# More warm-up products in the first head, fills behind the running sum, and new priorities in a planned attention and two-layer kernel

## The chip, the cores and the metric

The kernel runs on one core of a Trainium2 chip. The metric is the device time in microseconds (us) of one execution; lower is better. The engines are TensorE (PE, its weight loads PEld), VectorE (DVE), ScalarE (ACT), GpSimd (POOL) and SyncE (SP), which issues the DMAs.

## The reference

```python
def _attn_ref(q, k, v, s):                      # 4 batches, 8 heads, 576 positions, 64 per head
    scores = scale * np.matmul(q, k.transpose(0, 1, 3, 2))
    cum = np.cumsum(np.maximum(s, 0.0), axis=-1)
    bias = -(cum[:, :, :, None] - cum[:, :, None, :])
    scores = np.where(causal, -1000000000.0, scores + np.minimum(bias, 0.0))
    attn = np.exp(scores - np.max(scores, axis=-1, keepdims=True))
    attn = attn / (np.sum(attn, axis=-1, keepdims=True) + 1e-09)
    return np.matmul(attn, v)
# x: 2304 x 512
h = (x @ w1) * (x @ w2) @ w3;  y = h @ w_out    # 512 -> 1024 -> 512
h2 = y @ w_in;  out = (h2 - np.tanh(h2)) @ w_out2   # 512 -> 2048 -> 512
```

## The kernel before

**Stages.** Batch 0 comes first, its eight heads in plain fp32 (`full`). The 24 heads of the other batches work on fp32r pairs: a value is split into a high part (a copy) and a low part (a subtraction), and a product is three matmuls. The two products with w1 and w2 (`products`, six blocks of 384 tokens) are put between the heads as the results of whole batches come. Then w3 and w_out are multiplied into one weight matrix (`wah`, `wal`), which is applied to the tokens (the x2 stage), and last the layer with w_in, the tanh and w_out2 runs in blocks of 512 tokens (the last stage; 16 slices of the hidden size, f, in each).

**A head** has five query tiles (`QT`: 64 and four of 128 rows). For each: scores into one of two banks, a reduction on DVE that adds the mask and finds the maximum, an exponential on ACT, transposes on PE (`flip`), copies out of PSUM, and the product with v (`pv`). The bias enters as rows of the k side that hold the running sum relative to the tile's middle (`rel`): each head after the first gets them by DMA into `rqk`, five rows beside the 64 of k, and needs one matmul per piece. The first head multiplies q and k alone and adds the bias by a second matmul (ones by `rel`) into the same bank.

**The weights.** They arrive as 64-bit floats and are made into fp32 by one ACT step and four DVE steps for 128 x 512 values (`assemble`, lines 487 to 493), then split by a copy (line 385 on ACT, 386 on DVE) and a subtraction (389 on DVE, 391 on POOL). w1 and w2 are 16 such blocks. w_out2 is 16 more; four of them are assembled early, laid by in DRAM and fetched later (`lay_by`, `fetch`). Four blocks of w_out2 have room in the pool `pre`, which opens while the x2 stage still runs; the other twelve stand in `p2`, which opens when it ends.

**What sets the order.** A planner (`Plan.order`) gives each operation a start by its own estimates: at each moment an engine takes the ready operation with the smallest priority number, and operations that two engines can do (copies on ACT or DVE, subtractions on DVE or POOL) go where the planner expects the earlier end, with a handicap for each. The program is then written out in that order, and each engine runs its own list in order. All numbers of the table `PARAM` feed it: `convp` and `convq` are the priorities of the w1 and w2 blocks (a head's number is 100 times its place), `qk` and `kb` how early a head's loads are asked for, `dsub0`, `dcopy0` the handicaps of DVE for subtractions and copies in the first stretch. Where PE would stand idle before `fu`, the planner puts in warm-up products (`filler`: 128x128 bf16 on zeros, into a bank nobody reads).

## Time and profile before

| | |
|---|---|
| median of three runs | 961.36 us (957.67 to 964.69) |
| span of the profiled execution | 957.5 us; no other time of it is given, and the lowest run is 957.67 |
| PE busy | 941.5 us (98%) |
| DVE, ACT, POOL busy | 662.6, 594.8, 419.2 us |

The profile is one execution. A busy PE is not a PE at its peak, since the ends of matmuls are modelled: in the heads of batch 0, PE counts as busy nearly throughout but runs fewer matmuls in the same time than later. So the stretches are compared by several engines together, and with the granted clock.

### The profile page before, as it was taken

What the parts mean: (1) busy time and instruction counts of PE and PEld (TensorE: products, weight loads), DVE (VectorE), ACT (ScalarE), POOL (GpSimd) and SP (SyncE); (2) the same over time, 40 slices, a digit from 0 to 9 for tenths busy, and PEclk for the clock granted to TensorE, in tenths of its full rate; (3) what the DMA queues carried; (4) which work ended last, traced back from release to release, by engine and by line L of the source; (5) the groups of instructions that cost most, each with busy time, mean ns of one, the idle gap of its engine ahead of it and who ended that gap; (6) DMA issues with size and microseconds to landing.
All of it is one profiled execution on the core that took longest, in us unless ns stands there. A gap on an engine that the chain in (4) does not pass through costs nothing. (4 is left out here: it accounts for less than half of the span.)

```text
span 957.5 us, 15393 instructions
## 1 busy us (share of the span) xinstructions
PE 941.5 (98%) x5147; PEld 819.6 (86%) x5147; DVE 662.6 (69%) x1383; ACT 594.8 (62%) x1362; POOL 419.2 (44%) x337
## 2 busy tenths in 40 slices
PE   9997999999999999999999999999999999999998
PEld 5775999998999998899888887888888888888897
DVE  6998777678877579982588878894454544554555
ACT  4997677888898554441455468665555655655564
POOL 2445455645565254430687736453233233233321
PEclk7999999999999999999999999999999999999999
DMA  5655565565543145573598780121002101000010
GB/s 183 204 167 149 153 207 176 160 212 178 154 135 98 53 131 181 181 271 136 152 362 286 234 289 25 51 103 45 1 1 89 44 1 44 34 12 0 1 46 22
DMA packets 64305, 118.96 MB, mean 124 GB/s; under 512 B 6433, under 2 KB 34321, under 8 KB 64226
## 3 DMA queue, kind: packets, MB, share of 16 engines
q1 hardware_dynamic: 64226, 117.98, 38.6%
q8 instruction: 40, 0.66, 0.3%
q14 instruction: 39, 0.32, 0.1%
HBM read 88.81 MB, written 25.46 MB: 119 GB/s over the span
## 5 line engine op out<-in xcount | busy, mean ns | idle before, releaser
L391 POOL TENSOR_TENSOR gl<-pg,gh 128x512 fp32r<-128x512 f32 (+1 forms) x78 | 118.7, 1522 | 231.7 <-ACT gh L385 219.6
L933 PE MATMUL bank<-x2b,wih 128*128 128x512 f32 (+1 forms) x640 | 182.4, 370 | 0.0
L944 DVE TENSOR_TENSOR pg<-bank,u 128x512 f32<-128x512 f32 (+1 forms) x80 | 51.0, 637 | 138.9 <-ACT th L943 132.3
L933 PEld LDWEIGHTS bank<-x2b,wih 128*128 128x128 f32 x640 | 117.0, 188 | 22.1
L941 ACT ACTIVATE u<-bank 128x512 f32<-128x512 f32 (+1 forms) x80 | 44.4, 555 | 126.1 <-PE bank L933 125.9
L933 PE MATMUL bank<-x2b,wil 128*128 128x512 f32 (+1 forms) x320 | 117.9, 368 | 0.0
L956 PE MATMUL bank<-voh,gl 128*128 128x512 f32 x288 | 113.2, 393 | 1.7 <-POOL gl L391 1.6
L954 PE MATMUL bank<-voh,gh 128*128 128x512 f32 x288 | 113.0, 392 | 0.0
L955 PE MATMUL bank<-vol,gh 128*128 128x512 f32 x288 | 112.6, 391 | 0.0
L666 ACT ACTIVATE e<-e,nmx 128x320 f32<-128x320 f32 (+4 forms) x160 | 89.0, 559 | 16.0 <-DVE nmx L660 15.3
L698 PE MATMUL bank<-ident,e 128*128 128x128 f32 (+1 forms) x480 | 80.0, 278 | 3.9 <-ACT e L666 2.2
L660 DVE CUSTOM_DVE_ANT_0 e<-bank,msk 128x320 f32<-128x320 f32 (+4 forms) x160 | 65.8, 422 | 23.1 <-PE bank L650 13.4
L391 POOL TENSOR_TENSOR xl<-cf,xh 128x512 fp32r<-128x512 f32 (+1 forms) x40 | 55.3, 1409 | 47.4 <-ACT xh L385 45.1
L948 DVE COPY_PREDICATED pg<-mk,th 128x512 f32<-128x512 uint32 (+1 forms) x80 | 68.4, 856 | 8.5 <-ACT mk L946 1.4
L389 DVE TENSOR_TENSOR el<-bank,eh 64x64 fp32r<-64x64 f32 (+1 forms) x144 | 63.8, 458 | 12.1 <-ACT eh L385 11.3
L487 ACT ACTIVATE wt<-wraw 128x512 f32<-128x512 f32 x72 | 48.0, 669 | 34.6 <-DMA wraw<-w_out 13.0
L933 PEld LDWEIGHTS bank<-x2b,wil 128*128 128x128 f32 x320 | 60.2, 188 | 10.5
L493 DVE SCALAR_TENSOR_TENSOR wt<-wraw,wt 128x512 uint32<-128x512 uint32 x72 | 68.5, 953 | 0.9
L797 PE MATMUL bank<-xh,w1h 128*128 128x384 f32 x192 | 68.8, 358 | 0.1
L491 DVE SCALAR_TENSOR_TENSOR wt<-wraw,wt 128x512 uint32<-128x512 uint32 x72 | 67.5, 940 | 1.0
L797 PE MATMUL bank<-xh,w2h 128*128 128x384 f32 x192 | 67.6, 352 | 0.0
L698 PEld LDWEIGHTS bank<-ident,e 128*128 128x128 f32 (+1 forms) x480 | 56.5, 139 | 12.5 <-ACT en L385 2.8
(139 smaller groups left out, 2493.5 us busy)
## 6 DMA issues: line engine op xcount, KB each, us to landing
rqk<-qk SPq DMA_DIRECT2D x24, 576.0 KB
wraw<-w_out SPq DMA_DIRECT2D x24, 512.0 KB
c_d<-cst SPq DMA_DIRECT2D x48, 192.0 KB
wraw<-w SPq DMA_DIRECT2D x16, 512.0 KB
wraw<-w3t SPq DMA_DIRECT2D x16, 512.0 KB
wraw<-w_in SPq DMA_DIRECT2D x16, 512.0 KB
cf<-c_d SPq DMA_DIRECT2D x32, 256.0 KB
x_d<-x2s SPq DMA_DIRECT2D x16, 512.0 KB
```

The source lines that it names most:

```text
L391: o.append(("POOL", c_pool2(n), lambda: nc.gpsimd.tensor_tensor(dst(), a(), b().bitcast(F32), op=ALU.subtract)))
L491: dve(lambda: nc.vector.scalar_tensor_tensor(t_.t, h32(), 0xC0000000, t_.t, op0=ALU.bitwise_and, op1=ALU.bitwise_or), 512, [r_, t_], [t_], ...
L493: dve(lambda: nc.vector.scalar_tensor_tensor(t_.t, l32(), 29, t_.t, op0=ALU.logical_shift_right, op1=ALU.bitwise_or), 512, [r_, t_], [t_], ...
L660: nc.vector.tensor_tensor_reduce(e.t[:nq, EOFF[t] + k0:EOFF[t] + k1], bk.t[:nq, :k1 - k0], bi.t[:nq, bo + k0:bo + k1], -0.125, 3.0e38 if f ...
L666: act(lambda: nc.scalar.activation(et(), et(), AF.Exp, bias=nmx.t[:nq, i, tm:tm + 1], scale=-1.0, accum_out=ssum.t[:nq, pj, t, i:i + 1]), ...
L698: nc.tensor.transpose(bk.t[:rows, n * P:(n + 1) * P], e.t[:, EOFF[t] + c * P:EOFF[t] + c * P + rows], ident.t)
L797: nc.tensor.matmul(bk.t[:, :TB], w_.t[:, k, f * P:(f + 1) * P], x_.t[:, k, o:o + TB], start=k == 0 and i == 0, stop=k == KC - 1 and i == 2)
L933: nc.tensor.matmul(bk.t[:, :w], w_.t[:, k, a], X2.t[:, i, k, :w], start=k == 0 and n == 0, stop=k == KC - 1 and n == 2)
L948: dve(lambda pg=pg, mk=mk, th=th, c_=c_: nc.vector.copy_predicated(c_(pg), c_(mk).bitcast(U32), c_(th)), w, [mk, th], [pg], pr, two=True)
L954: nc.tensor.matmul(bank[n].t, gh.t[:, a], voh[f].t, start=f == 0, stop=False)
L955: nc.tensor.matmul(bank[n].t, gh.t[:, a], vol[f].t, start=False, stop=False)
L956: nc.tensor.matmul(bank[n].t, gl.t[:, a], voh[f].t, start=False, stop=f == NF2 - 1)
```

## The change

Five things. (1) `PARAM`: priorities and handicaps are other numbers, among them `convp` 581 to 1692.7 and `convq` 511 to 1648.5 (the w1 and w2 blocks rank behind the heads of batch 0), `lay0` 4 to 0 (slices 0 to 3 of w_out2 are laid by in DRAM, where it was 4 to 7) and `wlast` 12 to 6. (2) Warm-up products are planned at 55 ns where it was 107, and go into gaps from 60 ns where it was 110: 164 of them where it was 91. (3) Memory settings (`zero`) depend on the running sum, and the two of `rqk` are done by POOL. (4) The last two tiles of the first head take the bias as rows, like the other heads: their second matmuls go, and a DMA brings the rows. (5) The first half of the w1 and w2 blocks waits for the last of the five relative sums.

```diff
-PARAM = dict(ramp0=146, ramp1=-16.1, dsub=2038, dsub0=404, dcopy=753, dcopy0=203, dother=1000.0, dother0=1000.0, spi=420, lay=4, lay0=4, layp=2.2e5, layf=2.95e5, dve0=1000.0, early=140811, raw0=0, rawp=-700.0, ng=3, nosb=2, cut=(1,), convq=511, natb=8, wap=0.95e6, dve=1000.0, act=-188, pool=-128, sem=160.0, pesem=180.0, slow=1.1, convp=581, npre=4,
-             nbias=3, keep=0.5, ff=0.0, fu=174005, wlast=12, kbp=246, qk=-145, kb=-365, rv=116, st=9.8, fl=38, iv=174, pv=129, ml=-120, bw=370.0, ntr=3, actb=1, actn=0, spp=-44, ne=2, nsb=2, ncf=5, outlag=40)
+PARAM = dict(cst=1050.9, ramp0=113.5, ramp1=35.9, dsub=5134.3, dsub0=979.7, dcopy=723.0, dcopy0=29.4, dother=1000.0, dother0=1000.0, spi=1234.9, lay=4, lay0=0,
+             layp=263506, layf=214480, dve0=1000.0, early=154617, raw0=0, rawp=-700.0, ng=3, nosb=2, cut=(1,), convq=1648.5, natb=8, wap=842711, dve=1000.0,
+             act=-76.1, pool=-71.7, sem=160.0, pesem=180.0, slow=1.1, convp=1692.7, npre=4, nbias=3, keep=0.5, ff=0.0, fu=215099, wlast=6, kbp=469.5, qk=-461.8,
+             kb=-1288.7, rv=341.5, st=7.6, fl=112.8, iv=-82.0, pv=113.8, ml=-119.7, bw=370.0, ntr=3, actb=1, actn=0, spp=349.6, ne=2, nsb=2, ncf=5, outlag=119.8)
...
-                while self.fill_from < free[e] and free[e] + 110.0 < t < self.fill_until and not unread and free[e] >= read:
+                while self.fill_from < free[e] and free[e] + 60.0 < t < self.fill_until and not unread and free[e] >= read:
...
-                    f.dur = 107.0 * self.clock(free[e])
+                    f.dur = 55.0 * self.clock(free[e])
...
-    def zero(views, n, w, prio, value=0.0):
-        pl.op([("DVE", sum(0.521 * x + 75.0 for x in n), lambda: [nc.vector.memset(v_(), value) for v_ in views])], w=w, prio=prio, two=True)
+    def zero(views, n, w, prio, value=0.0, r=()):
+        pl.op([("DVE", sum(0.521 * x + 75.0 for x in n), lambda: [nc.vector.memset(v_(), value) for v_ in views])], r=r, w=w, prio=prio, two=True)
...
+    scan = [(rel, 5)]
...
+            zero([later(en, 1024, EN, low), later(en, 0, D, low)], [P, D], [en], 30, r=scan)
...
+            for R in rqk:
+                pl.op([("POOL", 560.0, lambda R=R: nc.gpsimd.memset(R.t[D:D + 5, S:], 0.0))], w=[(R, 2)], prio=-2300)
...
-            S, [(rel, 5)], [(rel, t)], -900 + t if t < 3 else 20.0 + t, fast=True)
+            S, [(rel, 5)], [(rel, t)], -900 + t, fast=True)
...
-        elif n_head[0] > 1:
-            for t0, t1 in ((0, 3), (3, 5)) if 1 in groups else ((0, 3),):
+        else:
+            for t0, t1 in ((3, 5),) if one else ((0, 3), (3, 5)) if 1 in groups else ((0, 3),):
...
-                    if one:
+                    if one and t < 3:
...
-                if one:
+                if one and t < 3:
...
-                        PARAM["convp"] + half * PARAM["convq"] + (2 * k + (src is w2)) * PARAM["ramp%d" % half], PARAM["rawp"] if half == 0 and 2 * k + (src is w2) < PARAM["raw0"] else None)
+                        PARAM["convp"] + half * PARAM["convq"] + (2 * k + (src is w2)) * PARAM["ramp%d" % half], PARAM["rawp"] if half == 0 and 2 * k + (src is w2) < PARAM["raw0"] else None,
+                        [(rel, 4)] if half == 0 and 2 * k + (src is w2) else [])
```

Line numbers of the changed kernel are up to five higher (the scores of later heads are 651 where they were 647), and the setup code has moved. Three places show what the planner makes of it.

PE, first head, from the third query tile to the first scores of the second head. Before: each piece of scores has a second matmul with `rel`; `rqk_103` holds the first head's q and k, `rqk_104` the second's; L698 are transposes, L738 the product with v.

```order
129 L644 MATMUL bank_58<-rqk_103 128x320
130 L645 MATMUL bank_58<-rel,e_114 128x320
131 L644 MATMUL bank_59<-rqk_103 128x448
132 L645 MATMUL bank_59<-rel,e_114 128x448
133 L698 MATMUL bank_61<-ident,e_113 64x128
134 L698 MATMUL bank_62<-ident,e_113 128x128 x2
135 L644 MATMUL bank_58<-rqk_103 128x288
136 L645 MATMUL bank_58<-rel,e_114 128x288
137 L644 MATMUL bank_59<-rqk_103 128x288
138 L645 MATMUL bank_59<-rel,e_114 128x288
139 L698 MATMUL bank_63<-ident,e_113 128x128 x3
140 L698 MATMUL bank_61<-ident,e_113 128x128 x4
```

Now (L548 is a warm-up product; of runs of them the last row stands here):

```order
214 L548 MATMUL bank_60<-msk 128x128
215 L648 MATMUL bank_58<-rqk_103 128x320
216 L649 MATMUL bank_58<-rel,e_114 128x320
217 L702 MATMUL bank_62<-ident,e_113 128x128 x2
218 L702 MATMUL bank_61<-ident,e_113 64x128
...
263 L651 MATMUL bank_59<-rqk_103 128x448
264 L651 MATMUL bank_58<-rqk_103 128x288
265 L702 MATMUL bank_63<-ident,e_113 128x128 x3
...
274 L651 MATMUL bank_59<-rqk_103 128x288
275 L742 MATMUL bank_60<-en,rv_106 80x320
...
278 L702 MATMUL bank_61<-ident,e_113 128x128 x4
279 L651 MATMUL bank_58<-rqk_104 128x64
```

The three second matmuls of the last two tiles are gone, 77 warm-up products stand ahead of the first scores (62 before), then 28 ahead of row 215, 22 ahead of row 263 and four ahead of row 274, and the second head's first scores come before the transposes of the first head's last tile.

DVE, the beginning. Before:

```order
8 L522 MEMSET rqk_103 5x576
...
10 L522 MEMSET rv_106 128x16
...
12 L522 MEMSET en 64x128
...
14 L571 TENSOR_SCALAR rel<-rel 32x576
15 L522 MEMSET e_114 128x64 x4
16 L572 SCALAR_TENSOR_TENSOR rel<-rel 32x576
...
18 L578 TENSOR_SCALAR rel<-rel 32x576 x3
19 L660 ISA e_113,nmx<-bank_58,msk 64x64
...
21 L578 TENSOR_SCALAR rel<-rel 32x576 x2
22 L660 ISA e_113,nmx<-bank_59,msk 128x192
```

Now:

```order
5 L524 MEMSET ssum 128x20
6 L555 TENSOR_SCALAR rel<-rel 32x576
7 L556 SCALAR_TENSOR_TENSOR rel<-rel 32x576
8 L582 TENSOR_SCALAR rel<-rel 32x576 x5
9 L524 MEMSET e_113 128x64 x4
10 L524 MEMSET en 64x128
...
12 L524 MEMSET e_113 64x64
13 L664 ISA e_113,nmx<-bank_59,msk 128x192
...
15 L664 ISA e_113,nmx<-bank_58,msk 64x64
```

The running sum (row 7) has no memory setting between it and its input, all five relative sums follow it at once, and the first reductions come behind them and behind four settings.

DVE, where the x2 stage ends and the last stage begins (`wt` is an assembled block of w_out2, `voh` its high part, L944 and L949 the first step of the last stage). Before, the cast is slice 8; slices 4 to 7 come by DMA:

```order
1024 L488 TENSOR_SCALAR wt_83<-wt_83 128x512
1025 L489 TENSOR_SCALAR wt_83<-wt_83 128x512
1026 L491 SCALAR_TENSOR_TENSOR wt_83<-wraw_81,wt_83 128x512
1027 L386 CAST voh_5697<-wt_82 128x512
1028 L944 TENSOR_TENSOR pg_5730<-bank_62,u_5724 128x512
```

Now the casts are slices 4 and 5, and slices 6 to 15 are all assembled behind this point:

```order
1024 L391 TENSOR_TENSOR x2s_4794<-bank_61,x2s_4794 128x256
1025 L388 CAST voh_5746<-wt_82 128x512
1026 L388 CAST voh_5747<-wt_83 128x512
1027 L949 TENSOR_TENSOR pg_5783<-bank_62,u_5777 128x512
...
1034 L490 TENSOR_SCALAR wt_82<-wt_82 128x512
```

On PE there, seven slices of the first product stand ahead of the first of the second, where it was six.

## Rows read from the trace of the kernel before

**Rows 1.** The page: span; busy time, share and instructions of each engine.

```profile
span 957.5 us, 15393 instructions
PE 941.5 (98%) x5147; PEld 819.6 (86%) x5147; DVE 662.6 (69%) x1383; ACT 594.8 (62%) x1362; POOL 419.2 (44%) x337
```

**Rows 2.** Windows: stretch, length, busy of PE, PEld, DVE, ACT, POOL, clock, DMA, GB/s.

```profile
11.84:22.08 10.24, 10.24 (x28) 5.30 (x26) 5.53 (x13) 5.11 (x13) 2.19 (x2) 0.50 0.41 104
22.08:81.94 59.86, 57.94 (x339) 43.59 (x338) 54.17 (x156) 53.88 (x157) 25.43 (x20) 1.00 0.63 186
81.94:97.17 15.23, 10.40 (x69) 8.45 (x68) 11.92 (x34) 11.24 (x38) 9.38 (x10) 0.89 0.40 107
97.17:340.00 242.83, 240.74 (x1732) 234.76 (x1730) 178.26 (x559) 192.00 (x542) 128.48 (x125) 1.00 0.50 151
560.00:600.00 40.00, 38.33 (x167) 30.66 (x166) 33.09 (x49) 31.95 (x57) 22.50 (x15) 1.00 0.39 133
600.00:957.50 357.50, 353.99 (x1637) 293.80 (x1635) 196.43 (x305) 202.06 (x380) 113.36 (x76) 1.00 0.09 33
```

**Rows 3.** Timeline of PE, first head: start us, length us, what, idle before.

```profile
6.49 0.32 PE L644 MATMUL bank<-rqk 64*64 64x64 f32 x2
...
9.67 0.80 PE L645 MATMUL bank<-rel,e 1*128 1x320 f32 x2
...
14.72 1.32 PE L645 MATMUL bank<-rel,e 1*128 1x288 f32 x2
...
20.34 2.03 PE L738 MATMUL bank<-en,rv 128*80 128x320 f32 x6
...
22.77 1.46 PE L647 MATMUL bank<-rqk 69*128 69x64 f32 x6
```

**Rows 4.** Timeline of DVE, first head.

```profile
5.27 0.33 DVE L522 MEMSET e<- 128x64 f32 x4
5.63 1.35 DVE L572 TENSOR_TENSOR_SCAN rel<-rel 32x576 f32<-32x576 f32 x1
...
8.74 0.94 DVE L578 TENSOR_SCALAR rel<-rel 32x576 f32<-32x576 f32 x2
...
16.46 1.34 DVE L389 TENSOR_TENSOR el<-rel,eh 64x1152 fp32r<-64x1152 f32 x1
...
18.59 0.52 DVE L660 CUSTOM_DVE_ANT_0 e<-bank,msk,nmx 128x288 f32<-128x288 f32 x1 [0.78 <-PE bank L645]
```

**Rows 5.** Groups of DVE, 0 to 81.94: count, busy us, mean ns, idle before.

```profile
L491 DVE SCALAR_TENSOR_TENSOR wt<-wraw,wt 128x512 uint32<-128x512 uint32 x16 | 12.0, 748 | 0.0
...
L488 DVE TENSOR_SCALAR wt<-wt 128x512 f32<-128x512 f32 x16 | 7.7, 488 | 0.8 <-ACT wt L487 0.5
```

**Rows 6.** Groups of ACT, 0 to 81.94.

```profile
L385 ACT ACTIVATE en<-bank 128x512 f32<-128x512 f32 (+3 forms) x47 | 17.6, 416 | 7.2 <-PE bank L698 4.5 <-PE bank L738 2.5
L487 ACT ACTIVATE wt<-wraw 128x512 f32<-128x512 f32 x16 | 10.6, 674 | 7.0 <-DMA wraw<-w 6.4 <-POOL w1l L391 0.5
```

**Rows 7.** Waits of PE over the whole span: total, times, longest us.

```profile
PE bank L698 <- ACT e L666: 2.2, 1, 2.2
PE bank L740 <- DVE el L389: 1.9, 1, 1.9
PE bank L956 <- POOL gl L391: 1.6, 1, 1.6
```

**Rows 8.** Timeline of DVE, 86 to 91.

```profile
87.15 2.58 DVE L389 TENSOR_TENSOR qs<-rqk,qs 64x320 fp32r<-64x320 f32 x1
```

**Rows 9.** Timeline of ACT, last stage: copies of a w_out2 block's high part.

```profile
588.84 0.64 ACT L385 ACTIVATE voh<-wt 128x512 fp32r<-128x512 f32 x1 [1.96 <-DVE wt L493]
...
640.72 0.63 ACT L385 ACTIVATE voh<-wt 128x512 fp32r<-128x512 f32 x1 [0.75 <-DVE wt L493]
```

**Rows 10.** Chain of waits, last stage: first product of two neighbouring slices.

```profile
590.04 2.75 PE bank L933 x12
595.55 2.73 PE bank L933 x12
```

More of the change, by code (lines that the diff above doesn't have):

```diff
@@ L528, in tile_kernel @@
     zero([lambda: fix.t[D:D + 5]], [S], [(fix, 1)], -2900, 1.0)
-    low = slice(D, P)
-    for e in e2[:1] + [en] + e2[1:]:
-        if e is en:
-            zero([later(en, 1024, EN, low), later(en, 0, D, low)], [P, D], [en], 30)
-            zero([lambda: ssum.t], [20], [ssum], -5, 1.0)
-            for R in rqk:
-                zero([lambda R=R: R.t[D:D + 5, S:]], [S], [(R, 2)], 5)
-        else:
-            zero([later(e, EOFF[0] + D, EOFF[0] + EW[0])] + [later(e, EOFF[t] + QT[t][1], EOFF[t] + EW[t]) for t in range(1, 5) if EW[t] > QT[t][1]],
-                 [D] * 4, [(e, range(4))], -10 if e is e2[0] else 92)
-            zero([later(e, EOFF[0], EOFF[0] + D, low)], [D], [(e, 0)], -10 if e is e2[0] else 92)
-    for V in rv:
-        zero([lambda V=V: V.t[:, 5 * D:]], [VW - D], [(V, 1)], 30)
-    for x in (eh, el):
-        zero([later(x, EB + 1024, ETOT, low), later(x, 0, D, low)], [P, D], [x], PARAM["kbp"] - 10)
-    zero([lambda: const.t[:, 0:1]], [1], [const], 5.0e4, SQ_B)
-    zero([lambda: const.t[:, 1:2]], [1], [const], 5.0e4, -T2)
     def patterns():
@@ L556, in constants @@
         for a in (D, D + 5):
-            dma(lambda a=a: q2[i].t[a:a + 5].bitcast(F32), lambda: fix.t[D:D + 5], 5 * S * 4, [(fix, 1)], [(q2[i], 1)], PARAM["kbp"] + 100, issue=830.0)
+            dma(lambda a=a: q2[i].t[a:a + 5].bitcast(F32), lambda: fix.t[D:D + 5], 5 * S * 4, [(fix, 1)], [(q2[i], 1)], PARAM["cst"], issue=830.0)
     dve(lambda: nc.vector.memset(msk.t[:, :D], 0.0), D, [], [(msk, 0)], -3000, fast=True)
@@ L572, in tile_kernel @@
     dve(lambda: nc.vector.tensor_tensor_scan(rel.t[2 * NH:, :S], rel.t[:NH, :S], rel.t[:NH, :S], 0.0, op0=ALU.add, op1=ALU.max), S, [(rel, 0)], [(rel, 5)], -1000, extra=650.0)
+    scan = [(rel, 5)]
+    low = slice(D, P)
+    for e in e2[:1] + [en] + e2[1:]:
+        if e is en:
+            zero([later(en, 1024, EN, low), later(en, 0, D, low)], [P, D], [en], 30, r=scan)
+            zero([lambda: ssum.t], [20], [ssum], -5, 1.0)
+            for R in rqk:
+                pl.op([("POOL", 560.0, lambda R=R: nc.gpsimd.memset(R.t[D:D + 5, S:], 0.0))], w=[(R, 2)], prio=-2300)
+        else:
+            zero([later(e, EOFF[0] + D, EOFF[0] + EW[0])] + [later(e, EOFF[t] + QT[t][1], EOFF[t] + EW[t]) for t in range(1, 5) if EW[t] > QT[t][1]],
+                 [D] * 4, [(e, range(4))], -10 if e is e2[0] else 92, r=scan)
+            zero([later(e, EOFF[0], EOFF[0] + D, low)], [D], [(e, 0)], -10 if e is e2[0] else 92, r=scan)
+    for V in rv:
+        zero([lambda V=V: V.t[:, 5 * D:]], [VW - D], [(V, 1)], 30, r=scan)
+    for x in (eh, el):
+        zero([later(x, EB + 1024, ETOT, low), later(x, 0, D, low)], [P, D], [x], PARAM["kbp"] - 10, r=scan)
+    zero([lambda: const.t[:, 0:1]], [1], [const], 5.0e4, SQ_B, r=scan)
+    zero([lambda: const.t[:, 1:2]], [1], [const], 5.0e4, -T2, r=scan)
     for t, (q0, q1) in enumerate(QT):
@@ L612, in head @@
             dma(lambda: KL.t[D:D + 10, :qb].bitcast(F32), lambda: kb_d.t[h, :, :, :qb].rearrange("n t s -> (n t) s"), 10 * qb * 4, [kb_d], [(KL, 1)], pr + PARAM["kb"])
-        elif n_head[0] > 1:
-            for t0, t1 in ((0, 3), (3, 5)) if 1 in groups else ((0, 3),):
+        else:
+            for t0, t1 in ((3, 5),) if one else ((0, 3), (3, 5)) if 1 in groups else ((0, 3),):
                 a, o = ROFF[t0]
```

## The prediction

> **What bounds the kernel now.** I read the page first: PE is busy 941.5 of 957.5 us [rows 1], so the time is PE's list and what idles in it. Then the windows by stage [rows 2]. From 97.17 to 340, PE idles 2.1 us of 242.8 and its weight loads fill 234.8. From 600 on it idles 3.5 of 357.5. Nothing much can be won there. What is loose lies at the front and at one seam. Between 22.08 and 81.94 (heads 1 to 7) PE counts as busy 57.9 of 59.9, but its weight loads fill only 73% where they later fill 97%, while DVE is busy 54.2 and ACT 53.9: two engines at 90% that feed PE. From 81.94 to 97.17 (the step to the split heads) PE idles 4.8 of 15.2. From 560 to 600 it idles 1.7, nearly all of it one wait of 1.6 for POOL's `gl` [rows 7]. And from 11.84 to 22.08, in the first head, the granted clock is 0.50, the lower of the two levels, 1.2 GHz [rows 2].
>
> The first head's chain is in the timelines. Its first scores start at 6.49, the second head's at 22.77 [rows 3]. A pair of bias matmuls over 320 columns takes 0.80 at the full clock, a pair over 288 columns takes 1.32 at half [rows 3]; by columns, 0.72 at full. DVE's last reduction starts at 18.59 after waiting 0.78 for PE's bias matmul [rows 4]: here PE is what DVE waits for.
>
> **First head.** (a) The memory setting of 0.33 ahead of the running sum goes [rows 4], so the sum starts near 5.3, ends at 6.65, and five relative sums at 0.47 (0.94 for two) end at 9.0 instead of 9.68. The first reductions come behind them and four settings (0.7 by the row of 0.33), near 9.7; the third tile's scores wait for the bank and are read near 12, 1 us later than now. POOL's two memory settings cost nothing: POOL is waiting then, and the rows that they fill are needed by a DMA that also needs the relative sums. (b) Three bias pairs go. At the trace's durations that is 1.32 twice and about 1.4 for the one of 448 columns (320 columns take 0.80, and it ends in the slow stretch), 4.0 us of PE; at full clock 0.72 twice and 1.1, so 2.6. (c) The rows for them come by a DMA issued near 9.8. It has until the 22 warm-up products ahead of those scores are through, near 13.8 (the third tile's scores and transposes at 12.4, and 22 at 0.06); not hidden, it would cost what it lands later. (d) If the 54 warm-up products between the tiles hold the clock up, the four pieces of scores and the product of 2.03 run at full clock. The chain then reads: fourth tile's scores 13.8 to 14.8, read behind DVE's subtraction of 1.34 [rows 4] by 15.6, last piece of scores at 15.7 to 16.4 and read from 16.5 (18.59 now), product with v 1.1, four transposes 0.45, second head's first scores at 18.0. That is 4.7 less than 22.77, of which five transposes are only moved behind (0.4). I take **-4.5**, ends -6 and 0: the 77 products ahead of the first scores, 15 more at 0.06, cost up to 0.9 if q and k land as early as now, but the relative sum is awaited there anyway.
>
> **Heads 1 to 7.** Counting the change's lists up to head 8's first reduction: DVE loses 12 of 62 assembly steps, six at 0.49 and six at 0.75 [rows 5], 7.4 us; three weight subtractions and the first splits of the next batch go too, about 3.5 by the nearest row, 0.75 each. It gains nine copies of `en` and seven other copies, at ACT's mean of 0.42 [rows 6] 6.7 us. ACT loses 12 copies of `en` (5.0), two assembly steps (1.3) and some copies, near 9 in all. So DVE sheds 4 and ACT 9 of about 54 each. At an unchanged 90% the stretch gets 4.4 shorter by DVE and more by ACT; PE's own idle there, 1.9, is the least that it could give if its pace is its own. I take **-3.5**, the nearer to DVE's end since DVE is the busier; ends 0 and -7.
>
> **Step to the split heads.** PE waits 2.2 there for an exponential and 1.9 for a DVE subtraction [rows 7]. The latter stood behind a DVE operation of 2.58 us on 64x320 [rows 8], more than three times an assembly step of 0.75 over 128x512 [rows 5]. The change puts six such subtractions of q and six of k on POOL by then, against four and two. On the other side three blocks of w1 and w2 are left to assemble there. I take **-2** of the 4.8 idle and of the clock's 0.89; ends +2 and -5.
>
> **Given back.** DVE's 7.4 us of assembly and their subtractions fall behind 81.94, where DVE idles 3.3 of 15.2 and later 64 of 243 [rows 2]; the products need them, and PE's list has 12 product matmuls ahead of head 8 where it had 18. **+1.5**, ends 0 and +4. POOL's list there grows from 34 to 44 operations. Over 0 to 81.94 DVE's two assembly rows average 0.75 and 0.49 [rows 5]; what POOL adds to them I put at **+1**.
>
> **Seam to the last stage.** Seven slices of the first product instead of six stand ahead of the wait for `gl`: 2.75 more cover [rows 10] for 1.6 of wait. **-1.5**, ends 0 and -1.7. Four slices of w_out2 are assembled behind the seam instead of ahead of it. That costs nothing in the forecast, since DVE has 161 us free behind 600 [rows 2] and slices are wanted one in 5.5 us [rows 10]. Laying by other slices, the two late groups of w3 (`wlast`) and the new numbers of the middle cost nothing either: PE idles there under 1%, and its list holds the same matmuls.
>
> **Sum.** -4.5 -3.5 -2 +1.5 +1 -1.5 = -9, so the profiled execution goes from 957.5 to 948.5. The median of the runs is 961.4, 3.9 above the profiled span, and I set the same 9 against it: **952**.
>
> **Rivals.**
> *POOL holds DVE up.* DVE's row of 2.58 us [rows 8] shows that an operation can stand several times its length. If each of the ten more POOL operations holds one DVE step for the time by which the longest row exceeds its neighbours' 0.75, halved, 0.9 us, DVE loses 9 and the gain of heads 1 to 7 and of the step is gone: -4.5 -1.5 +1.5 = -4.5, **957**. For it: DVE is the engine at 90%. Against it: most steps now run near 0.5 to 0.75 with POOL busy 25 of 60 us. The Trainium skill (SBUF — State Buffer, Who interferes with whom) states this as a rule: DVE and GpSimd share a pair of ports as an exclusive lock held for the whole instruction, so the loser blocks. By that rule the trace's one long row is such a block. Chance 0.24.
>
> *The clock falls all the same*, so the change doesn't do what its first words say. Then the scores, product and transposes of (d) run at half: 1.0, 0.7, 0.7, 1.1 and 0.45 double, +4, and the first head gives 0.5 or less: **956** with the rest, 960 with half of it. For it: it stood at half after 11.84 with PE counted busy throughout the next stretch [rows 2]. Chance 0.14; I put it at 957.
>
> *The weights of the last stage come too late: slower.* Six blocks of w_out2 took from 588.84 to 640.72, 10.4 us each [rows 9], and PE wants one in 5.5 [rows 10]. Before, slice 15 was ready at 641. Now ten blocks follow the seam at 576; at 10.4 the last is ready at 680, where the second product wants it near 580 + 15 x 5.5 = 662. PE would stand 18 us: 961 - 9 + 18 = **970**. It decides where a block takes over 8.6 us (86 for ten). For it: the rate is a row. Against it: DVE was not full then, slices were asked for late, and the change's list has slice 8 assembled by the sixth slice's elementwise steps. Chance 0.08.
>
> *All of it comes*: ACT's 9 counts, the step's idle goes too. -6 -6 -4 +1 -1.5 = -16 at most; I put it at -14, **947**. Chance 0.08.
>
> **Numbers.** The forecast (952, own range 948 to 956) has 0.46. About 1%, 9.6 us, is what tells a change from none here: below 951.7 is faster, above 971 slower. Faster: a little over half of the forecast (0.25, its middle lies at the bound), all of the last case (0.08), and the low ends of the POOL and the clock case (0.05 and 0.04), 0.42. Slower: 0.06 from the late weights and 0.03 for stalls that I don't see, 0.09. The rest, 0.49, is within. The range reaches from the case of all gains to the clock's with its worst end: 944 to 963, which leaves out most of the late weights and little else.
>
> **What would show it.** First head: second head's first scores near 18, granted clock 1.00 from 12 to 22. Heads 1 to 7: the first split head's scores near 74 instead of 81.94. Step: no DVE operation over 2 us, PE idle under 3. Seam: no wait of L961 for `gl`. Wrong would be: half clock in the first head, DVE's assembly steps on average above 0.8, or waits of L959 for `voh` or `vol` behind the seam.

## The result

The changed kernel took **951.41 us**, the median of 4 runs (950.12 to 952.06), where the kernel before, beside it, took 960.29 (957.67 to 964.69). The ratio is 0.9904, with a 95% interval of 0.9876 to 0.9933: faster by 0.9%, a little under the 1% that the prediction took as its bound. The profiled execution spans 948.4 us.

The page of the changed kernel, the two lines of [rows 1]:

```profile
span 948.4 us, 15455 instructions
PE 936.3 (99%) x5214; PEld 822.9 (87%) x5214; DVE 686.5 (72%) x1399; ACT 595.1 (63%) x1329; POOL 416.5 (44%) x354
```

The windows of the changed kernel, cut where [rows 2] are cut (stretch, length, busy of PE, PEld, DVE, ACT, POOL, clock, DMA, GB/s); the step to the split heads is two windows here, since the clock falls inside it:

```profile
17.83:73.01 55.18, 54.53 (x339) 41.93 (x338) 50.46 (x155) 48.80 (x140) 26.79 (x22) 1.00 0.67 200
73.01:82.70 9.69, 7.82 (x56) 6.44 (x54) 8.38 (x19) 7.07 (x24) 8.79 (x9) 1.00 0.61 183
82.70:92.94 10.24, 6.48 (x26) 5.84 (x26) 9.67 (x23) 6.84 (x23) 7.94 (x9) 0.50 0.28 75
92.94:340.00 247.06, 246.60 (x1770) 242.22 (x1769) 182.79 (x573) 187.59 (x525) 135.06 (x132) 1.00 0.50 150
560.00:600.00 40.00, 40.00 (x176) 32.72 (x175) 37.85 (x54) 29.12 (x50) 17.91 (x12) 1.00 0.19 67
600.00:948.40 348.40, 344.78 (x1597) 286.23 (x1595) 208.69 (x301) 206.11 (x374) 94.47 (x75) 1.00 0.10 34
```

The half clock has left the first head and now sits in the step, in a window where PE is busy 6.5 of 10.2 us.

PE's timeline in the first head (start, length, what, idle before) answers to [rows 3]:

```profile
6.95 0.33 PE L648 MATMUL bank<-rqk 64*64 64x64 f32 x2
...
8.50 1.74 PE L548 MATMUL bank<-msk 128*128 128x128 bf16 x28
...
12.02 1.39 PE L548 MATMUL bank<-msk 128*128 128x128 bf16 x22
13.25 1.46 PE L651 MATMUL bank<-rqk 69*128 69x448 f32 x4
...
17.83 0.71 PE L651 MATMUL bank<-rqk 69*128 69x64 f32 x4
```

The second head's first scores come at 17.83 instead of 22.77. The 28 and 22 fillers (the warm-up products of L548) take 62 ns each and stand where the planner expected PE to wait. The scores of 448 columns carry their bias as rows (69 partitions) and no pair for it follows.

DVE's timeline there, against [rows 4]:

```profile
3.23 1.71 DVE L556 TENSOR_TENSOR_SCAN rel<-rel 32x576 f32<-32x576 f32 x1
4.97 2.56 DVE L582 TENSOR_SCALAR rel<-rel 32x576 f32<-32x576 f32 x5
...
16.59 0.52 DVE L664 CUSTOM_DVE_ANT_0 e<-bank,msk,nmx 128x288 f32<-128x288 f32 x1
```

The running sum starts 2.4 us earlier and all five relative sums are through at 7.5. The prediction had moved one memory setting of 0.33 us from ahead of the sum and put its start near 5.3; in the change's order the others that stood there went behind it too, or to POOL. The last reduction no longer waits for PE.

PE's waits over the span (total, times, longest), against [rows 7]:

```profile
PE bank L654 <- DMA q<-fix: 4.0, 1, 4.0
PE bank L746 <- DVE eh L388: 1.5, 1, 1.5
PE bank L651 <- DVE nmx L664: 1.2, 2, 0.6
```

All three waits of [rows 7] are gone. Two new ones stand together in the step, 5.5 us of them.

To see where the 9.1 us of span came from, a stage has to be cut at the same piece of work in both traces. The first split head's scores won't do: they come at 73.01 instead of 81.94, but six product matmuls that stood ahead of them now stand behind. Product matmul number 30 and the first H product do. First the kernel before, then the changed one:

```profile
98.37 0.34 PE L797 MATMUL bank<-xh,w1h 128*128 128x384 f32 x1
...
554.63 0.63 PE L933 MATMUL bank<-x2b,wih 128*128 128x512 f32 x2
```

```profile
86.39 0.29 PE L654 MATMUL bank<-kl,q 74*64 74x64 f32 x1 [4.01 <-DMA q<-fix]
...
93.54 0.34 PE L801 MATMUL bank<-xh,w1h 128*128 128x384 f32 x1
...
547.66 0.63 PE L938 MATMUL bank<-x2b,wih 128*128 128x512 f32 x2
```

| stretch | before | after | difference | forecast |
|---|---|---|---|---|
| start to second head's first scores | 22.77 | 17.83 | -4.94 | -4.5 |
| heads 1 to 7 and the step, to product matmul 30 | 75.60 | 75.71 | +0.11 | -3.5 -2 +1.5 +1 = -3.0 |
| middle, to the first H product | 456.26 | 454.12 | -2.14 | 0 |
| seam and last stage, to the end | 402.88 | 400.75 | -2.13 | -1.5 |

Each column is one execution, and two of the rows need the spread of others beside them. The first: the second head's first scores come 10.88 us behind the head's own first scores, which came at 6.95 (6.49 before, where it was 16.28). All eight traces with this front (the change, e6, e8, e9, f3, g1, g2, g3 below) have 10.88 to 10.90, but their own starts lie from 6.95 to 8.21, so the first row would read -3.7 to -4.9 by the trace that one takes; without the start it is -5.4. The third: in the nine traces with the change's order (the change, f1, f2, f3, f5, g1, g2, g3, and e6 up to there) the middle took 454.1 to 459.1, so -2.14 between two executions is within chance.

### The profile page after: what moved, and what is told of

Its sections match the earlier page's. It is cut to its first block, busy times and chain, and to the rows that moved or that the text cites. A ratio compares the mean times of both kernels' runs of the same rounds, so it can differ in the third digit from the quotient of the medians.

```text
span 948.4 us, 15455 instructions
## 1 busy us (share of the span) xinstructions
PE 936.3 (99%) x5214; PEld 822.9 (87%) x5214; DVE 686.5 (72%) x1399; ACT 595.1 (63%) x1329; POOL 416.5 (44%) x354
## 4 chain that ended last, share of the span: by engine, by line
PE 95%; DVE 3%; ACT 1%; issue 1%; DMA 0%; POOL 0%; SPq 0%; DVEq 0%
PE bank L801 21%; PE bank L938 21%; PE bank L961 7%; PE bank L959 7%; PE bank L960 7%; PE bank L702 5%; PE bank L901 3%; PE bank L899 3%; PE bank L900 3%; PE bank L744 2%; PE bank L654 2%; PE bank L653 2%; PE bank L746 2%; PE bank L861 2%; PE bank L651 2%; PE bank L863 2%
## 5 line engine op out<-in xcount | busy, mean ns | idle before, releaser
L393 POOL TENSOR_TENSOR gl<-pg,gh 128x512 fp32r<-128x512 f32 (+1 forms) x78 | 99.9, 1280 | 254.5 <-ACT gh L387 247.7
L949 DVE TENSOR_TENSOR pg<-bank,u 128x512 f32<-128x512 f32 (+1 forms) x80 | 50.4, 630 | 90.4 <-POOL gl L393 86.3
L387 ACT ACTIVATE gh<-pg 128x512 fp32r<-128x512 f32 (+1 forms) x80 | 47.0, 588 | 99.2 <-PE bank L960 95.8
L952 DVE TENSOR_TENSOR th<-bank,th 128x512 f32<-128x512 f32 (+1 forms) x80 | 50.7, 634 | 45.9 <-ACT th L948 45.8
L953 DVE COPY_PREDICATED pg<-mk,th 128x512 f32<-128x512 uint32 (+1 forms) x80 | 78.2, 978 | 2.5 <-ACT mk L951 0.9
L702 PE MATMUL bank<-ident,e 128*128 128x128 f32 (+1 forms) x480 | 75.3, 274 | 0.5 <-DVE el L391 0.5
L495 DVE SCALAR_TENSOR_TENSOR wt<-wraw,wt 128x512 uint32<-128x512 uint32 x72 | 72.5, 1007 | 0.8
L493 DVE SCALAR_TENSOR_TENSOR wt<-wraw,wt 128x512 uint32<-128x512 uint32 x72 | 71.8, 997 | 1.0
L938 PEld LDWEIGHTS bank<-x2b,wil 128*128 128x128 f32 x320 | 60.3, 188 | 10.6
L391 DVE TENSOR_TENSOR el<-bank,eh 64x64 fp32r<-64x64 f32 (+2 forms) x144 | 62.6, 458 | 8.3 <-ACT eh L387 7.0
L951 ACT ACTIVATE mk<-u,const 128x512 f32<-128x512 f32 (+1 forms) x80 | 54.1, 676 | 18.8 <-DVE pg L953 18.5
```

Source lines behind the costliest of these rows:

```text
L393: o.append(("POOL", c_pool2(n), lambda: nc.gpsimd.tensor_tensor(dst(), a(), b().bitcast(F32), op=ALU.subtract)))
L493: dve(lambda: nc.vector.scalar_tensor_tensor(t_.t, h32(), 0xC0000000, t_.t, op0=ALU.bitwise_and, op1=ALU.bitwise_or), 512, [r_, t_], [t_], ...
L495: dve(lambda: nc.vector.scalar_tensor_tensor(t_.t, l32(), 29, t_.t, op0=ALU.logical_shift_right, op1=ALU.bitwise_or), 512, [r_, t_], [t_], ...
L702: nc.tensor.transpose(bk.t[:rows, n * P:(n + 1) * P], e.t[:, EOFF[t] + c * P:EOFF[t] + c * P + rows], ident.t)
L938: nc.tensor.matmul(bk.t[:, :w], w_.t[:, k, a], X2.t[:, i, k, :w], start=k == 0 and n == 0, stop=k == KC - 1 and n == 2)
L953: dve(lambda pg=pg, mk=mk, th=th, c_=c_: nc.vector.copy_predicated(c_(pg), c_(mk).bitcast(U32), c_(th)), w, [mk, th], [pg], pr, two=True)
```

## The experiments

Twelve kernels were run. The difference to the changed kernel is taken from the ratios to the kernel before, times 960.8, since each batch had its own runs of that; with two intervals in it, it is good to some 3.5 us. The span is of one execution.

| kernel | median, us | ratio to before, 95% | against the change | span |
|---|---|---|---|---|
| the change | 951.41 | 0.9904 [0.9876, 0.9933] | | 948.4 |
| f1, no gap fillers | 954.01 | 0.9908 [0.9886, 0.9929] | +0.4 | 952.0 |
| f2, bias products back | 955.09 | 0.9950 [0.9924, 0.9975] | +4.4 | 951.9 |
| f5, both | 957.58 | 0.9975 [0.9957, 0.9992] | +6.8 | 960.3 |
| e3, old numbers | 956.39 | 0.9933 [0.9913, 0.9952] | +2.8 | 954.6 |
| e4, old code, new numbers | 961.77 | 1.0020 [1.0004, 1.0035] | +11.1 | 958.8 |
| e8, one number moved | 956.13 | 0.9941 [0.9918, 0.9964] | +3.6 | 955.4 |
| e9, moved the other way | 959.48 | 0.9997 [0.9980, 1.0014] | +8.9 | 956.7 |
| e6, old `lay0` | 951.75 | 0.9906 [0.9883, 0.9928] | +0.2 | 951.3 |
| f3, one transfer | 950.69 | 0.9872 [0.9849, 0.9896] | -3.1 | 949.9 |
| g1, fillers in the step | 950.78 | 0.9895 [0.9874, 0.9917] | -0.9 | 947.6 |
| g2, f3 and DVE for POOL | 951.01 | 0.9903 [0.9879, 0.9928] | -0.1 | 949.2 |
| g3, g2 and fillers | 949.87 | 0.9889 [0.9873, 0.9906] | -1.4 | 948.2 |

### The first head

These three keep the changed kernel's order to the instruction: the plan is made as in the change, and some of it is left out or written otherwise as it is emitted.

**f1**: the 54 fillers between the first head's products are dropped.

```diff
+            n += self.done[i].prio == 9e9
+            if self.done[i].prio != 9e9 or not 76 < n <= 130:
-            self.done[i].fn()
+                self.done[i].fn()
```

> The changed kernel in its own order, without the 54 warm-up products between the tiles of the first head (28, 22 and 4); all others stay. If they hold the clock up: granted clock 0.50 for 7 to 10 us inside 8 to 22 us, the second head's first scores 1.5 to 4 us later than 17.83, and 2 to 4 us more at the end (953.5 to 955.5). Rival: the tiles wait for DVE and nothing of PE's pace shows: first scores within 0.5 of 17.83, 951 to 952.

PE's timeline in f1:

```profile
11.21 2.66 PE L654 MATMUL bank<-rqk 69*128 69x448 f32 x4
...
19.32 0.95 PE L654 MATMUL bank<-rqk 69*128 69x64 f32 x3
```

The clock stood at half from 10.6 to 20.8, and the two pieces of scores (448 and 288 columns) took 2.66 us where they take 1.46. So the fillers do hold the clock. But the second head is only 1.5 us later (1.7 from the first scores on), since the fillers also hold PE up: without them PE waits 0.72 us ahead of the third tile's scores, where the 28 take 1.74, and not at all ahead of the fourth's, which start 2.0 us sooner (11.21 against 13.25; 0.2 of it is this execution's earlier start). From there on the half clock costs 3.5. At product matmul 30 the delay is 0.85; the step's half clock lasts 6.8 us in f1 instead of 10.2. The 3.6 us at the end of the span hold 1.3 of a wait at 444 us that has nothing to do with the first head (below). By the ratios f1 is not told from the change.

**f2**: the bias of the last two tiles by products again, in the change's order.

```diff
-                    if one and t < 3:
+                    if one:
```

> The changed kernel in its own order, with the three bias matmuls of the first head's last two tiles put back (the DMA of the rows still runs, unread). If they lay on the chain: second head's first scores 1.4 to 2.6 us later than 17.83 and the end with them, 952.8 to 954. Rival: hidden behind DVE's subtraction of 1.34 and the reductions: under 0.5, 951 to 952.

Second head's first scores at 22.22, 4.4 later, which is over the 1.4 to 2.6 expected. Of that, 1.1 is a later start of this execution (first scores at 8.07 instead of 6.95), 2.5 the three products at full clock (1.01, 0.75 and 0.75), the rest the clock, which fell to half at 20.2. At product matmul 30 and at the end it is still 3.5 late, 1.1 of it that start: this one carries through.

**f5**: both.

> The changed kernel in its own order, with neither the 54 fillers between the first head's products (as f1_no_gap_fill) nor the bias as rows of the first head's last two tiles (as f2_bias_back). Alone they cost 2.6 and 3.7 us of the median, 3.6 and 3.5 us of the span. Theory A, that they are two shares, the clock and the three products: together 6 to 7 us, a median near 957.7, so that the first head alone holds two thirds of the change's 9 us; the second head's first scores near 24 us. Theory B, that they share the half clock (without fillers the three products run in it as well, and the wait that they take away is the one that the fillers fill): the second head's first scores come at 22.5 us or before, and the loss is under 5 us, a median under 956.4.

Second head's first scores at 23.65, 5.8 late, where f1 and f2 add to 5.9. Counted from the first scores on, it is 5.8 against 1.7 and 3.3: together they cost 0.8 more than alone, since in f5 the bias products run at half clock (1.86, 1.32 and 1.32 instead of 1.01, 0.75 and 0.75). So there are two shares, as theory A had it, and the median meets its 957.7; by the ratios, 6.8 against 0.4 and 4.4. From first to second head it takes 16.66, no less than the 16.28 before: with fillers and bias rows undone, the sum that comes 2.4 us earlier shows no gain of its own. The span's 11.9 is more than the first head: 6.9 late at matmul 30, and then the wait at 450 us, 1.9 us, after which the clock was at half for 3.4.

### Code and numbers

**e3**: the changed program with the numbers of before (and `cst=346`, what its formula gave).

```diff
-PARAM = dict(cst=1050.9, ramp0=113.5, ramp1=35.9, dsub=5134.3, dsub0=979.7,
+PARAM = dict(cst=346, ramp0=146, ramp1=-16.1, dsub=2038, dsub0=404,
...
```

> The changed code with the table of numbers of the kernel before. If the first head's gain is the code's (warm-up products, bias rows, settings behind the sum): second head's first scores within 1.5 us of 17.83, and 955 to 957; the new numbers then give the other 4 to 5 us. Rival: the table does it all: first scores over 21, 959 to 961.

Second head at 16.92, earlier than in the change. Yet product matmul 30 comes at 100.57, later than before the change (98.37): PE waited 5.8 us for the constants' transfer in the step, and the clock fell there for 10.2. The first head's gain of 5.8 was lost whole in one stage.

**e4**: the other half, before's program with the new numbers (the diff's two halves exchanged).

> The program before, with the numbers of the change alone (the priorities, lay0=0 and the others; its sum, its bias products and its fillers of 110 ns stay as they were). Theory A, that code and numbers are two shares that add: the new program with the old numbers ended 2.9 us before the program before in the profiled execution, the change 9.1 us, so this one ends about 6 us before it, near 951.5 us of span; the second head's first scores stay late, 21 to 23 us, since sum and bias products are the old ones. Theory B, that the numbers were chosen for the new program and are worth little with another: within 2 us of the span before, 955.5 to 959.5.

No faster than before: theory B. As a whole the numbers hold nothing by themselves. That leaves two readings of the 2.8 us between e3 and the change: that the numbers suit the new program, or that any order gives some other time. Two kernels ask that.

**e8** and **e9**: the change with one number moved, which computes the same in another order.

```diff
-             act=-76.1, pool=-71.7,
+             act=-80.0, pool=-71.7,
```

```diff
-             act=-76.1, pool=-71.7,
+             act=-72.0, pool=-71.7,
```

> The changed kernel with one number of the planner moved by a little (its estimate for ScalarE, act, from -76.1 to -80.0), which puts the instructions of TensorE in another order from the second head on and changes no computation. It shows how far a new order alone moves the time. Theory A, that what the change gave is the sum, the bias rows and the fillers in the first head and a broad gain of the order behind it: within 1.5 us of the changed kernel's span of 948.4. Theory B, that several of the 9 us are one good order among many: 2 to 6 us over it, 950.4 to 954.4. The second head's first scores are at 17.8 us in both.

> The changed kernel with the planner's number for ScalarE moved by a little to the other side (act from -76.1 to -72.0; e8_null moved it to -80.0 and cost 4.7 us of the median and 7.0 of the span). The first head stays as it is; from its end on the order is another one and there are 56 fillers more. Theory A, that the number sits on a good order by choice and its neighbours are worse: 953 to 958 us. Theory B, that e8_null was a chance miss in the middle and a new order usually keeps the gain: 950 to 952.5 us.

In both, the second head's first scores came as in the change (18.55 and 17.96, 10.9 behind the first scores). e8 then lost 3.6 us by the ratios, just what these can tell; e9 lost all of the gain. e8 was 1.3 behind at matmul 30 and 7.0 at the first H product; e9 6.5 and 8.3. Part of e8's loss is at one place. ACT's timeline, then PE's:

```profile
436.67 0.63 ACT L387 ACTIVATE xh<-cf 128x512 fp32r<-128x512 f32 x1 [4.87 <-DMA cf<-c_d]
437.20 0.47 ACT L387 ACTIVATE asb<-bank 128x384 f32<-128x384 f32 x1
```

```profile
437.73 0.44 PE L801 MATMUL bank<-xh,w1h 128*128 128x384 f32 x1 [2.41 <-ACT asb L387]
```

ACT stands 4.87 us on a copy whose transfer is not in. The copy that empties a bank is queued behind it, and PE waits 2.41 for that bank; the clock then falls for 3.4 us. In the change ACT waits 1.62 for the same transfer and PE not at all. In e6, f1 and f5, with the change's order up to there, ACT waited 2.82, 3.44 and 3.83, and PE 0.7, 1.3 and 1.9. So this place gives 0 to 2 us of wait in one and the same order, and f5's middle is as long with it (459.1) as e8's (459.8): e8's trace doesn't tell a worse order from a worse chance.

Most of e9's loss is in the step: from the first split head's scores to product matmul 30 it takes 26.4 us, where the change takes 20.5. There stand 51 of the 56 fillers that e9 has more, some 3 us of PE (windows of e9):

```profile
80.00:100.00 20.00, 15.10 (x119) 12.93 (x119) 17.11 (x44) 11.91 (x35) 17.41 (x17) 0.83 0.40 106
```

POOL is busy 17.4 of 20 us there, against 14.2 in the change. Which of the two makes the loss was not tried.

**e6**: the change with `lay0=4`, which leaves its order as it is up to the first H product.

```diff
-PARAM = dict(cst=1050.9, ..., lay=4, lay0=0,
+PARAM = dict(cst=1050.9, ..., lay=4, lay0=4,
```

> The changed kernel with lay0=4 as before, so that the order is the changed kernel's up to the seam (TensorE's first H products, 547.7 us) and differs from there on. Theory A, that lay0=0 is what took away TensorE's wait of 1.6 us for gl at the seam: the wait comes back and the span is 1 to 2.5 us longer than 948.4, the median 952.4 to 954. Theory B, that the wait went because the last stage starts 7 us earlier in another order anyway: no wait over 0.5 us between 548 and 620 us and the time within 0.7 us of the changed kernel's.

Theory B: the time is the change's, and no wait for `gl` came back. PE asks for its first gated products 16.35 us behind the first H product in e6, as before; in the change it is 19.07, the seventh slice. What differs is POOL's list. Its timeline before, where PE waited 1.6 us at 581.90, then in e6 and in the change:

```profile
578.41 1.74 POOL L391 TENSOR_TENSOR vol<-wt,voh 128x512 fp32r<-128x512 f32 x1
580.11 3.17 POOL L391 TENSOR_TENSOR gl<-pg,gh 128x512 fp32r<-128x512 f32 x2
```

```profile
581.58 1.30 POOL L393 TENSOR_TENSOR gl<-pg,gh 128x512 fp32r<-128x512 f32 x1 [5.78 <-ACT gh L387]
```

```profile
575.74 1.29 POOL L393 TENSOR_TENSOR gl<-pg,gh 128x512 fp32r<-128x512 f32 x1 [5.24 <-ACT gh L387]
```

Before, `gl` stood behind subtractions of the weights' low parts (`vol`) on a POOL that was busy nearly without a gap from 572 us. In the other two POOL waits over 5 us for `gh`: it has those subtractions behind it or still ahead. With six slices or seven, PE finds `gl` ready. The same holds of e3 (all the old numbers, six slices) and e4 (the old program, seven): no wait of PE for `gl` in either, and 400.8 and 400.6 us from the first H product to the end. All 13 traces but the one before have 400.6 to 400.8 there, where that has 402.9. So neither the numbers nor the program took the wait away; the order before happened to have it.

### The step

**f3**: in the change's order, the second pair of constants goes by one transfer, from the first pair, instead of two from `fix`.

```diff
+                if not i:
+                    nc.sync.dma_start(q2[0].t[a:a + 5].bitcast(F32), fix.t[D:D + 5])
+                elif a == D:
+                    nc.sync.dma_start(q2[1].t[D:D + 10].bitcast(F32), q2[0].t[D:D + 10].bitcast(F32))
```

> The changed kernel in its own order, but the constant rows of the second split buffer come in one DMA from the first buffer instead of two from the pattern tile. If the wait of 4.0 us for that DMA at the step to the split heads is a loss of its own: wait under 2.5 us, no half clock or a shorter one behind it (10.24 us of it now), 3 to 6 us less at the end (945.5 to 948.5). Rival: another transfer or the splits come as late, the wait only changes its name: 950 to 952.

DVE's timeline in f3, then PE's:

```profile
81.75 3.02 DVE L491 TENSOR_SCALAR wt<-wt 128x512 uint32<-128x512 uint32 x1
84.81 1.87 DVE L493 SCALAR_TENSOR_TENSOR wt<-wraw,wt 128x512 uint32<-128x512 uint32 x1
```

```profile
88.20 0.64 PE L658 MATMUL bank<-kh,qs 128*128 128x320 f32 x1 [3.65 <-DVE nmx L669]
```

The wait of 4.0 us for the transfer became one of 1.2 for a later transfer and one of 3.65 for DVE. An operation that took 0.41 at 88.35 took 3.02 at 81.75, while POOL ran the subtraction of `kl`, the two products of `xf` and one subtraction of `vs` with no gap over 0.1 us. From the first split head's scores to product matmul 30 it took 21.03 us, no less than the change's 20.53, and the median lies in the rival's range: the transfer was not what the step hung on. (The -3.1 of the ratio is within what two intervals leave open, and the span is 1.5 us longer.)

**g2**: f3, with five of POOL's operations of the step given to DVE (two 64x320 subtractions, the two products of `xf`, the subtraction of `xl`).

```diff
+            (self.done[i].opts["DVE"][1] if j in (707, 713, 717, 719, 729) else self.done[i].fn)()
```

> The kernel f3_one_const (the changed kernel's order, the second pair of constants by one transfer), with five operations of the step on VectorE that GpSimd had: the subtractions of qs (GpSimd: 0.87 us at 80.50) and kl (0.86), the two products of xf (1.72 together) and the subtraction of xl (1.85 at 84.95). VectorE gets some 2 us of work more (its 64x320 subtraction of an earlier tile took 0.47, its 128x512 ones 0.7), and GpSimd leaves it free between 80.5 and 84.3 us. Theory A, that VectorE was held up by GpSimd there (L491 3.02 us where it takes 0.42 alone, L493 1.87 where it takes 0.7): these come down to under 0.6 and under 0.9, the wait of 3.65 us for nmx falls under 2 us, no. 30 comes 1.5 to 3 us earlier than in f3 (94.18) and the span is 1 to 3 us under its 949.9. Theory B, that the wait is one for the data (the scores' operands, the rows of x): the operations get short, the wait stays over 3 us under another name and the span is within 0.7 us of 949.9.

DVE's timeline in g2, then PE's:

```profile
83.78 0.43 DVE L491 TENSOR_SCALAR wt<-wt 128x512 uint32<-128x512 uint32 x1
...
84.53 0.68 DVE L493 SCALAR_TENSOR_TENSOR wt<-wraw,wt 128x512 uint32<-128x512 uint32 x1
```

```profile
88.88 0.63 PE L658 MATMUL bank<-kh,qs 128*128 128x320 f32 x1 [2.48 <-DVE nmx L669]
```

The same two operations, 4.89 us in f3, take 1.11 with POOL still. That POOL held them is shown. But DVE's own list is longer now, it has no gap to speak of from 78 to 92 us, and the wait only falls to 2.48. From the first split head's scores to product matmul 30 it is 19.50 us, against 21.03 in f3 and 20.53 in the change; the time is no shorter. The clock stood at half for 6.8 us in g2 and 10.2 in f3, so the 1.5 us can be the clock's alone. Neither theory fits whole: the operations got short, and something else took their place.

**g1**: the change's order with 72 fillers in the two waits of the step.

```diff
+            self.pad = {709: 20, 730: 52}.get(j, 0)
...
+        for _ in range(pl.pad):
+            nc.tensor.matmul(bk.t[:, :P], x, x, start=True, stop=True)
```

> The changed kernel in its own order, with 20 filler products in front of the product with V at 81.26 us (TensorE waits 1.46 us there) and 52 in front of the split head's scores at 82.19 us (it waits 4.01 us behind them), into the banks that these write next. A filler took 62 ns in the first head, so they fit into the waits (1.2 and 3.2 us). Theory A, that the half clock from 82.7 to 93.0 us is a loss of its own: the clock stays at 1.00, the 6.6 us of products between 86.4 and 93.0 us take 3.5 to 4.5, product matmul no. 30 comes at 91 to 92 us (93.54) and the span is 2 us shorter, near 946.5. Theory B, that TensorE is fed by a VectorE that GpSimd holds up and by nothing else there: the clock stays up, but TensorE waits for scores' reductions instead; no. 30 comes at 93 us or later and the span is within 0.7 us of 948.4.

PE's timeline in g1:

```profile
82.74 3.08 PE L553 MATMUL bank<-msk 128*128 128x128 bf16 x52
85.63 0.22 PE L659 MATMUL bank<-kh,qs 128*64 128x64 f32 x1
```

The clock stays at 1.00 through the step. The stretch takes 18.57 us, 2.0 less than in the change: theory A for the stretch. The other traces of this order agree, since the stretch goes by how long the clock stood at half: 18.9 and 19.2 us where it was 6.8 (f2, f1), 20.5, 21.0, 21.1 and 21.5 where it was 10.2 (the change, f3, f5, e6). The span is 0.8 shorter, 1.4 if this execution's later start is taken off (first split head's scores at 73.57), a little short of A's 2.

**g3**: g2 with 62 fillers.

```diff
+            self.pad = {709: 18, 730: 20, 731: 24}.get(j, 0)
+            (self.done[i].opts["DVE"][1] if j in (707, 713, 717, 719, 729) else self.done[i].fn)()
```

> g2_dve_subs (one transfer for the second pair of constants, five operations of the step on VectorE) with fillers in its three waits of the step: 18 in front of the product with V (1.45 us of wait), 20 in front of the split head's first scores (1.46) and 24 in front of its second (the third tile waits 2.48 us behind it). Theory A, that the half clock and the held VectorE are two shares: g1_step_fill kept the clock at 1.00 and took 2.0 us out of the stretch from the first split head's scores to product no. 30 (18.57 us, 20.53 in the changed kernel), g2_dve_subs 1.0 (19.50), both together some 3 (17.5), and the median is 948 to 949.5. Theory B, that behind the fillers VectorE, busy without a gap from 78 to 92 us in g2_dve_subs, sets the time: the stretch stays over 18.5 us and the median is 950 or more.

PE's timeline in g3:

```profile
88.15 0.42 PE L664 MATMUL bank<-kh,qs 128*128 128x320 f32 x1 [2.10 <-DVE nmx L675]
```

Full clock, but the stretch takes 18.66, no better than g1: theory B for the stretch. With the clock held, taking POOL's work over buys nothing, since DVE has to do it. The median of 949.87 lies between the two theories. It is the lowest of the medians, and is still not told from the change's.

## Why the total was right and half of its terms were not

**First head, forecast -4.5, measured -4.94 (-3.7 to -4.9 by the trace taken): right, with its mechanism but for the sum.** Three pairs gone, full clock, last reduction at 16.59 where 16.5 was said, second head at 17.83 where 18.0 was said. The sum came at 3.23, 2 us sooner than said, but f5 shows no gain by it. What f1, f2 and f5 add is the shares: the bias products are worth most and carry through; of the clock's 1.5 us, 0.85 is left at product matmul 30.

**Heads 1 to 7, the step and what is given back, forecast -3.0, measured +0.1: the terms that failed.** The marks that the prediction set for the heads came out, and misled. The first split head's scores were due near 74 and came at 73.01: heads 1 to 7 up to there took 55.18 us instead of 59.17, -4.0 where -3.5 was said. But six products had moved behind that mark, and the step from there to product matmul 30 took 20.53 instead of 16.43, +4.1 where -2 +1.5 +1 = +0.5 was said. From the second head's first scores to the first moved product (80.81 before, 75.96 now) it is 58.04 and 58.13 us. PE idled less there (0.65 us instead of 1.92) and ran 361 matmuls instead of 328, but 23 of the 33 more are fillers, and the rest is mainly six split scores that now stand ahead and five moved transposes: some wait was filled, and work changed places. In the step the forecast was -2, by the two waits that would go. They went, 2.2 and 1.9, and waits of 4.0 and 1.5 came, with the half clock: 10.24 us of it where before had 3.4. So the sign of PE idle under 3 us failed (5.6 of 20.53), while that of no DVE operation over 2 us came (the longest took 1.91). I had asked what the waits of [rows 7] were for, and not what PE would wait for once it came 9 us sooner: the constants, whose last two transfers are issued at 80.37 and 83.00 instead of 84.68 and 87.63, 4.3 and 4.6 us sooner only, and DVE's steps. g1 prices the clock's part at 2 us. What else holds the step is open: f3 and g2 show a wait for DVE, first held by POOL and then full, but with the clock held the stretch is as long with that relief (18.66 in g3) as without it (18.57 in g1), and part of the +4.1 is the moved work.

So the rival that **POOL holds DVE up** happens in this stage, if it doesn't set the whole. In heads 1 to 7 it shows less. DVE's groups of the changed kernel from 0 to 73.01 (count, busy us, mean ns, idle before), against [rows 5]:

```profile
L493 DVE SCALAR_TENSOR_TENSOR wt<-wraw,wt 128x512 uint32<-128x512 uint32 x12 | 10.5, 874 | 0.0
L495 DVE SCALAR_TENSOR_TENSOR wt<-wraw,wt 128x512 uint32<-128x512 uint32 x12 | 9.2, 767 | 0.0
L490 DVE TENSOR_SCALAR wt<-wt 128x512 f32<-128x512 f32 x13 | 6.5, 502 | 0.0
L491 DVE TENSOR_SCALAR wt<-wt 128x512 uint32<-128x512 uint32 x13 | 5.9, 451 | 0.0
```

The other two of the four before, from 0 to 81.94:

```profile
L493 DVE SCALAR_TENSOR_TENSOR wt<-wraw,wt 128x512 uint32<-128x512 uint32 x14 | 10.9, 779 | 0.1
L489 DVE TENSOR_SCALAR wt<-wt 128x512 uint32<-128x512 uint32 x16 | 6.5, 418 | 0.0
```

The mean of all four is 0.64 us where it was 0.60, under the 0.8 that the prediction named as a sign; only the two long ones lie above it together (0.82, and 0.76 before). At the old means the 50 steps would have taken 2.0 us less, where +1 was forecast. The Trainium skill (SBUF — State Buffer, Who interferes with whom) says that of the two engines one holds the ports for a whole instruction and the other blocks; the 3.02 us beside POOL in f3 and the 0.43 without it in g2 agree that it blocks. In f3 the block lasted over four of POOL's instructions in a row, not one.

**Middle, forecast 0, measured -2.14.** "PE idles there under 1%" is true, and leaves room for all of it: PE idled 2.15 of 456 us there before, in six gaps, of which these are the three longest (waits of PE, between 155 and 222 us):

```profile
PE bank L698 <- DVE el L389: 0.6, 1, 0.6
PE bank L742 <- DVE xf L749: 0.6, 1, 0.6
PE bank L698 <- ACT rinv L385: 0.4, 1, 0.4
```

In the change 0.57 of idle is left, so 1.6 of the 2.14 are waits that went. Whether they went for good is not shown: in the change's order this stage took 454.1 to 459.1 us by the execution, and before has only this one trace.

**Seam, forecast -1.5, measured -2.13: the wait went, for another reason.** The seventh slice was to cover it. e6 and e3 have six and no wait. POOL no longer had `gl` behind weight subtractions in the change. e3 and e4 show that neither the old numbers nor the old program bring the wait back by themselves: it belonged to the one order before.

**Late weights**, the slower rival: the view of waits lists none of PE after 540 us, and the ten blocks' copies run from 568.52 to 633.43, 7.2 us apart, under the 8.6 from which it would have decided. **The clock falls all the same**: not in the first head, but it did in the step.

So -9 came out as -4.9, +0.1, -2.1 and -2.1. Only the first was foreseen in place, size and cause. That the sum met the forecast is luck: the 3 us that failed in the step were made up by 2.1 in the middle, which was forecast at nothing and which chance can give, 0.6 at the seam and 0.4 in the first head. By e9, another order can lose the whole gain again, and it lost most of it in the step.

## What to carry to other kernels

Where numbers set a planner's order, an edit's price is read with the order held: leave the plan as it is and drop or rewrite single operations as they are emitted. And move one number by a little, to see what a new order alone does; here that was 4 us, just told from none, and 9 us, as much as the whole gain. Before a stage's difference gets a cause, look how much that stage differs between traces of one order; here the middle's 2.1 us was less than that. A gain at the front counts only as far as the next place where something else sets the pace: cut both traces at the same piece of work, not at a stage's name, and ask what the engine that comes sooner will find not ready.

## What the runs showed of the hardware that I had not expected

- A DVE step of 0.41 us (128x512, in place) took 3.02 in f3 with POOL running beside it, seven times as long, and 0.43 at the same place in g2 with POOL still.
- Fillers put into waits that were there anyway kept the granted clock at 1.00 (2.4 GHz): 72 of them (g1) took 2 us out of the step. Those in the first head ran past the waits: they held PE up by some 2 us and gave 3.5 (f1). Without the 72 the clock fell to 0.50 at 82.70, 0.3 us into a wait of 4.0 that followed one of 1.5.
- In one and the same order, ACT's wait for the transfer of `cf` was 1.23 to 3.83 us in nine traces (1.62 in the change), and the first scores of these came from 6.73 to 8.21 us. Single spans of this kernel that differ by 1 to 2 us say little.
